# Two transformer and mixer layers on one core: key norms of four head groups in one bank, a third score bank for odd exponential units, score buffers as a ring, and a new order

## The chip, the core and the metric

The kernel runs on one core of a Trainium2 chip. A core has five engines with instruction queues of their own: TensorE (PE; its weight loads are shown as PEld), VectorE (DVE), ScalarE (ACT), GpSimd (POOL) and SyncE (SP), which here issues most of the DMA transfers. Each engine works through its own instructions in the order in which the program has them; between engines there are semaphores. TensorE writes to PSUM, which has eight banks of 128 partitions by 512 float32 numbers. The other memory on the core is SBUF.

The metric is device time in microseconds (us) of one execution, the median of several runs. Before the change it is 1029.02 us over three runs (1027.13 to 1029.56).

## What is computed

Input is one sequence of 2048 tokens with 448 features. A step is an attention block and then a mixer block, each added to its input; two such steps follow each other with the same weights. Called layer 0 and layer 1 below, they are cut here to what matters:

```python
def _A_ref(x, wqkv, wo):                     # 16 heads of 28 columns
    q, k, v = split(x @ wqkv)
    scores = einsum("bhqd,bhkd->bhqk", q, k) * (Dh ** -0.5)
    p = softmax(scores, axis=-1)
    return reshape(einsum("bhqk,bhkd->bhqd", p, v)) @ wo

def _B_ref(x, w1, w2, w3, w4):
    h = gelu(layernorm(x) @ w1)              # 448 columns, in four quarters
    hs = shifted by -1, +1, -2, +2 tokens per quarter @ w2
    x1 = x + hs
    return x1 + gelu(layernorm(x1) @ w3) @ w4   # w3: 448 to 1792

x = x + _A_ref(layernorm(x), wqkv, wo)
x = x + _B_ref(layernorm(x), w1, w2, w3, w4)
x = x + _A_ref(layernorm(x), wqkv, wo)
x = x + _B_ref(layernorm(x), w1, w2, w3, w4)
```

The exponentials of the softmax are 2 layers x 16 heads x 2048 x 2048.

## The kernel before

**Who sets the order.** The kernel isn't written as a list of instructions. Each piece of work is a Python generator (a task) that yields operations, waits for named events, and asks for resources such as a PSUM bank. While the kernel is built, a planner (`Sched`) runs all tasks against planned durations, picks the next operation for each engine, and so fixes each engine's order; `Plan` turns the data dependences into semaphore waits. On the chip the order is fixed, and only the waits decide when an instruction starts. The choices of the planner are steered by tables of constants in the middle of the file: `RANK` (priority of projections, mixer steps and so on), `R_RATE` and `D_RATE` (how many score blocks go to VectorE in which part of the work), `Q_LEAD`, `PE_NORM`, and `XPAR` (thresholds, and by step whether VectorE or GpSimd does it). Where the planner sees TensorE idle, `keep_pe_busy` puts filler matmuls (`filler`, L2165) that compute nothing.

**Tiling.** Tokens are cut into 16 tiles of 128. Four heads form a group, each in 32 of 128 partitions, so there are four head groups. Queries go in chunks of four tiles (512 columns), the last two chunks of each layer in two tiles. `segs` lists the pairs of a query chunk and a head group with a range of key tiles. A segment's scores are cut into blocks of 128 keys by 512 columns (for chunks of two tiles: two key tiles by 256). Over both layers there are 2048 blocks, in the order of the list `stream`.

**The score pipeline.** `t_scores` takes the blocks off the stream in units. An even unit has up to three blocks and the banks 0 to 2, an odd one two blocks and the banks 3 and 4 (`unit_banks`). The scores are row-packed matmuls (L1416). `t_exp` turns a unit into one ScalarE activation (L1654) over all of its banks, into the bf16 buffer `PT` of 15 slots of 512 columns. The planner lets unit u start its scores when the exponential of unit u - 2 has ended. A block's slot is fixed by its unit's number,

```python
home[blk] = ("pt", 5 * ((u // 2) % 3) + 3 * (u % 2) + len(un))
```

so slots are used again after six units, and the exponential of unit u waits until the blocks of unit u - 6 have been used up. Some blocks aren't ScalarE's: in place of an even unit's third block (`ahead_of` with `R_RATE`), or beside a unit in a free bank (`D_RATE`), a later block of the stream is computed by VectorE, as a polynomial with bit operations in five instructions (L1498, two steps at L1525 and L1527, then L1529 and L1532), into `PD` or borrowed space in `vaug`. `t_pv` multiplies the probabilities with the values (L825 is the helper's line for these matmuls), and accumulates in bank 5, which it keeps from start to end. For all other matmuls (projections, mixer, norms; helper line L834) the tasks ask `misc` for one of the banks 6, 7 and 5; bank 5 being held, that leaves 6 and 7. After the last exponential ("tail") all banks are open to them.

**Key norms.** The softmax isn't shifted by the true maximum of a row, but by a bound from the norms of queries and keys. For each layer, each key chunk (`KC`: four chunks in layer 0, five in layer 1) and each head group, `k_proj` projects the keys into a bank, VectorE evacuates them into `kT` (L1182), the squares are formed in `sq` (L1168, on GpSimd or VectorE), one matmul set with `astat` sums them per head in another bank, and VectorE takes the maximum over the tokens (L1195) into `kmaxc`. `t_bias` and `t_bias4` make the biases of the query rows from it (L1325 to L1349). Chunk 0 of layer 0 takes the squares with ScalarE (L1165), for a quick start.

**Other ScalarE work.** The gelus of the mixer: as table gelu in long activations that come after loads of another function table (L2118 for the 1792-wide one, L1916 for the 448-wide one), or, for some chunks, as tanh (L1934), which needs no table load beside exp, with steps on GpSimd and VectorE around it (L1932, L1933, L1935). In the tail the gelus are taken straight from PSUM (L2090, L1898).

**Small steps that are named below.** L2018: GpSimd or VectorE adds the mixer's inner residual. L1763: the attention output is scaled. L1246, L1217, L1438: query rows are evacuated and given their bias. L1262: the values are evacuated into `vaug`. L2149: the output is evacuated into `obf`, two buffers, and stored by a DMA.

Of the kernel before, what the change touches and what calls it, by code (L numbers as in the profile page):

```python
# [184 lines left out]
class Sched:  # L185
# [140 lines left out]
    def keep_pe_busy(self, until):  # L326
# [8 lines left out]
        while True:  # L335
# [21 lines left out]
            if pick is None:  # L357
                if not fits:
                    break
                if self.open5 and all(d.t_end + 0.2 <= t for d in self.P.deps("pe", reads, [key("b5")]).values()):  # L360
                    f_ = self.P.add("pe", lambda e: fn(e, "b5"), reads + [(("xn", 0), "pad")], [key("b5")], t_end=t + dur)
# [190 lines left out]
R_RATE = {(0,): 0, (1,): 0.17, (2,): 0.183, (3,): 0.152, (4,): 0, (5,): 0, (6,): 0.274, (7,): 0.096, (8,): 0.106, (9,): 0.193, (10,): 0.073, (11,): 0.196, (12,): 0.228, (13,): 0, (14,): 0, (15,): 0.457, (16,): 0.306, (17,): 0, (18,): 0, (19,): 0.082, (20,): 0, (21,): 0.089, (22,): 0, (23,): 0.481, (24,): 0, (25,): 0.086, (26,): 0.053, (27,): 0.007, (28,): 0.051, (29,): 0.263, (30,): 0.207, (31,): 0.244, (32,): 0, (33,): 0.012}  # L552
# [3 lines left out]
DWIN = 3.0  # L556
# [5 lines left out]
RANK = {('q', 0, 1): 1, ('q', 0, 2): 1.763, ('q', 0, 3): 1.176, ('q', 1, 0): 1.162, ('q', 1, 1): 1.21, ('q', 1, 2): 1.085, ('q', 1, 3): 1.967, ('b', 0, 0): 3, ('b', 0, 1): 2.77, ('b', 0, 2): 1.853, ('b', 0, 3): 2.798, ('b', 0, 4): 1.211, ('b', 1, 0): 2.781, ('b', 1, 1): 1.849, ('b', 1, 2): 2.32, ('b', 1, 3): 2.579, ('b', 1, 4): 2.042, ('a', 0, 0): 1.98, ('a', 0, 1): 1.742, ('a', 0, 2): 1.882, ('a', 0, 3): 1.528, ('a', 0, 4): 2.263, ('a', 1, 0): 2.618, ('a', 1, 1): 1.108, ('a', 1, 2): 1.44, ('a', 1, 3): 1.223, ('a', 1, 4): 1.214, ('k', 0, 1): 2.594, ('k', 0, 2): 2.273, ('k', 0, 3): 2.136, ('k', 1, 0): 2.166, ('k', 1, 1): 1.68, ('k', 1, 2): 1.231, ('k', 1, 3): 2.338, ('k', 1, 4): 2.507, ('c', 0, 0): 1.464, ('c', 0, 1): 1, ('c', 0, 2): 2.866, ('c', 0, 3): 2.39, ('c', 0, 4): 1.764, ('c', 1, 0): 1.835, ('c', 1, 1): 1.44, ('c', 1, 2): 2.171, ('c', 1, 3): 2.127, ('c', 1, 4): 2.53, ('w', 0, 0): 2.816, ('w', 0, 1): 1.099, ('w', 0, 2): 2.277, ('w', 0, 3): 2.222, ('w', 0, 4): 1.537, ('w', 1, 0): 1.87, ('w', 1, 1): 2.531, ('w', 1, 2): 2.03, ('w', 1, 3): 2.877, ('w', 1, 4): 3, ('o', 0, 0): 2.728, ('o', 0, 1): 1.549, ('o', 0, 2): 1.72, ('o', 0, 3): 1.329, ('o', 0, 4): 2.769, ('o', 1, 0): 2.974, ('o', 1, 1): 3, ('o', 1, 2): 1.615, ('o', 1, 3): 1.476, ('o', 1, 4): 1.611, ('v', 0, 1): 1.389, ('v', 0, 2): 2.811, ('v', 0, 3): 3, ('v', 1, 0): 2.33, ('v', 1, 1): 1.844, ('v', 1, 2): 1, ('v', 1, 3): 1.537, ('v', 1, 4): 2.768, ('l', 1, 0): 1.014, ('l', 1, 1): 1.661, ('l', 1, 2): 2.714, ('l', 1, 3): 2.867, ('l', 1, 4): 1.565}  # L562
Q_LEAD = {(0, 1): 14, (0, 2): 51, (0, 3): 92, (1, 0): 95, (1, 1): 20, (1, 2): 92, (1, 3): 88}
# [36 lines left out]
def build_kernel(nc, A_x, A_wqkv, A_wo, B_x, B_w1, B_w2, B_w3, B_w4, out, n_layers=2):  # L600
# [79 lines left out]
    with st:  # L680
# [489 lines left out]
        def k_proj(L, c, g, xt):  # L1170
# [366 lines left out]
        def t_scores():  # L1537
# [40 lines left out]
            while True:  # L1578
# [32 lines left out]
                if not un:  # L1611
                    break
# [655 lines left out]
```

## Time and profile before

| | |
|---|---|
| median of three runs | 1029.02 us |
| the profiled execution, device time | 1027.56 us |
| its span, from the first to the last instruction | 1025.8 us |
| granted TensorE clock | 1.000 |
| exponentials on ScalarE (L1654) | 356 of 1536 columns, 435 of 1024 |
| first exponential starts, last ends | 16.2 us, 972.7 us |
| filler matmuls (L2165) | 2648 and 644, busy 121.4 and 30.4 us |

Times in the profile are from the span's start. A group's row has line, engine, operation, output and inputs, shape and count, then busy time and the mean of one in ns, then the engine's idle time just ahead of them and what ended it. Busy time counts overlapping instructions once, the mean counts each in full; ScalarE's activations overlap at their ends. A row of the timeline has start, length, group and count, and in brackets the idle time before it and what ended it. A row of the waits has who waited, for whom, the total, the number of times and the longest.

### The profile page before, as it was taken

The numbers are of one execution on the slowest core, as the hardware profiler recorded it, in microseconds if no ns is written. First come the engines' busy times: TensorE is split into PE (matmuls) and PEld (weight loads), VectorE is DVE, ScalarE is ACT, GpSimd is POOL, SyncE is SP. The second block draws the span as 40 slices with busy tenths as digits, with TensorE's granted clock in tenths as the row PEclk, the third lists the DMA queues.
The fourth block names the chain that finished last, engine by engine and source line by source line (L and its number), as shares of the span: only waits on it lengthen the run. The fifth ranks groups of instructions, "written<-read, shape, count | busy, mean of one in ns | idle before, by whom it ended". The sixth has DMA issues, their size and how long they took to land.

```text
span 1025.8 us, 35791 instructions
## 1 busy us (share of the span) xinstructions
PE 973.6 (95%) x16053; PEld 403.7 (39%) x16053; DVE 830.9 (81%) x1616; ACT 982.3 (96%) x903; POOL 255.0 (25%) x370
## 2 busy tenths in 40 slices
PE   8999999999999999999999999999999999899998
PEld 3333344333343334434334333333334333344465
DVE  7977899989869787878788778898999787787652
ACT  7999999999999999999999999999999999999942
POOL 2124132433134204342233111012313020231120
PEclk9999999999999999999999999999999999999999
DMA  4433453311104003231132015334212111121000
GB/s 121 118 90 103 126 166 89 60 33 38 24 26 98 18 14 100 54 54 24 27 91 77 12 62 161 102 73 120 59 29 38 23 47 41 33 64 36 13 21 24
DMA packets 98808, 64.38 MB, mean 63 GB/s; under 512 B 70816, under 2 KB 87536, under 8 KB 98656
## 3 DMA queue, kind: packets, MB, share of 16 engines
q1 hardware_dynamic: 95280, 54.02, 20.4%
q0 software_dynamic: 3376, 8.09, 2.9%
q8 instruction: 125, 2.05, 0.9%
q14 instruction: 27, 0.22, 0.1%
HBM read 28.16 MB, written 16.76 MB: 44 GB/s over the span
## 4 chain that ended last, share of the span: by engine, by line
ACT 73%; PE 23%; DVE 3%; DMA 0%; issue 0%; SPq 0%; DVEq 0%
ACT PT L1654 65%; PE ps L834 13%; PE ps L1416 5%; PE ps L825 4%; ACT h2T L2118 3%; ACT fb L1934 1%; ACT L1654 1%; PE ps L2165 1%; ACT L2118 1%; DMA PT<-in_A_wqkv_dram 0%; ACT sq L1165 0%; ACT vaug L2118 0%; DVE ub L1738 0%; ACT hT L1916 0%; DVE qT L1217 0%
## 5 line engine op out<-in xcount | busy, mean ns | idle before, releaser
L1654 ACT ACTIVATE PT<-ps 128x1024 bf16<-128x1024 f32 (+1 forms) x791 | 887.0, 1316 | 5.4 <-PE ps L1416 4.1
L1416 PE MATMUL ps<-qT,kT 32*128 32x512 bf16 (+1 forms) x2560 | 309.0, 340 | 27.6 <-ACT PT L1654 19.4
L825 PE MATMUL ps<-PT,vaug 128*32 128x512 bf16 (+1 forms) x2428 | 242.4, 341 | 0.1
L1416 PEld LDWEIGHTS ps<-qT,kT 32*128 32x128 bf16 x2560 | 79.3, 91 | 297.3 <-ACT PT L1654 271.1
L834 PE MATMUL ps<-xT,w 128*32 128x512 bf16 (+4 forms) x2592 | 178.6, 343 | 2.8 <-DVE hT L1903 1.5
L2165 PE MATMUL ps<-ident 128*32 128x256 bf16 x2648 | 121.4, 277 | 1.8 <-POOL ident L919 1.5
L825 PEld LDWEIGHTS ps<-PT,vaug 128*32 128x32 bf16 x2428 | 72.0, 95 | 85.8 <-issue 72.6
L834 PEld LDWEIGHTS ps<-xT,w 128*32 128x32 bf16 (+1 forms) x2592 | 69.9, 95 | 53.8 <-issue 24.6
L834 PE MATMUL ps<-w,h2T 128*32 128x448 bf16 x1288 | 86.2, 355 | 4.1 <-ACT h2T L2118 4.0
L2165 PEld LDWEIGHTS ps<-ident 128*32 128x32 bf16 x2648 | 76.3, 97 | 25.7 <-issue 9.9
L1498 DVE TENSOR_SCALAR yd<-ps 128x512 int32<-128x512 f32 x85 | 58.4, 687 | 20.2 <-PE ps L1416 19.1
L2094 DVE CAST h2T<-ps 128x384 bf16<-128x384 f32 (+1 forms) x84 | 51.9, 618 | 24.4 <-PE ps L834 23.7
L1763 POOL TENSOR_TENSOR otn<-ub,fb 128x512 bf16<-128x512 f32 (+1 forms) x24 | 29.4, 1227 | 127.1 <-DMA fb<-rscr 115.1
L1527 DVE SCALAR_TENSOR_TENSOR fb<-fb,yd 128x512 f32<-128x512 f32 x81 | 60.3, 748 | 0.6
L1525 DVE SCALAR_TENSOR_TENSOR fb<-yd 128x512 f32<-128x512 uint16 x81 | 59.6, 741 | 0.5
L1532 DVE SCALAR_TENSOR_TENSOR PD<-yd,PD 128x512 int16<-128x512 int16 x80 | 56.5, 709 | 1.0
L834 PEld LDWEIGHTS ps<-w,h2T 128*32 128x32 bf16 x1288 | 33.7, 96 | 33.2 <-issue 12.4
L1168 POOL TENSOR_TENSOR sq<-qT 128x512 bf16<-128x512 bf16 x20 | 24.4, 1221 | 85.3 <-DVE qT L1217 85.3
L1168 POOL TENSOR_TENSOR sq<-kT 128x512 bf16<-128x512 bf16 (+2 forms) x24 | 22.9, 955 | 90.6 <-DVE kT L1182 62.4
L834 PE MATMUL ps<-xT,wk_pad 128*32 128x512 bf16 (+1 forms) x512 | 42.8, 369 | 0.1
L834 PE MATMUL ps<-wo_pad,otn 128*32 128x448 bf16 x512 | 38.0, 355 | 2.0 <-DVE x_res L1818 1.6
L2007 POOL TENSOR_SCALAR mst<-mv 128x1 f32<-128x1 f32 x32 | 8.5, 268 | 123.7 <-DVE mv L1021 111.4
(210 smaller groups left out, 1319.7 us busy)
## 6 DMA issues: line engine op xcount, KB each, us to landing
uscr<-ub SPq DMA_DIRECT2D x28, 256.0 KB
ub<-uscr SPq DMA_DIRECT2D x28, 256.0 KB, 3.1
fb<-rscr SPq DMA_DIRECT2D x96, 64.0 KB, 2.0
xnd<-xn SPq DMA_DIRECT2D x28, 128.0 KB, 2.0
x_res<-in_A_x_dram POOLq DMA_DIRECT2D x16, 224.0 KB, 4.3
xd<-x_res SPq DMA_DIRECT2D x16, 224.0 KB, 2.2
x_res<-xd SPq DMA_DIRECT2D x16, 224.0 KB, 2.7
out_dram<-obf SPq DMA_DIRECT2D x16, 112.0 KB, 1.7
```

Source lines behind the costliest of these rows:

```text
L825: return lambda e: e.matmul(out=out, lhsT=lhsT, rhs=rhs, start=start, stop=stop, **kw)
L834: r.append(e.matmul(out=out[c:c + w, :], lhsT=lhsT[:, c:c + w], rhs=rhs, start=start, stop=stop, tile_position=(0, c)))
L1168: return both(kp, 0.15 + NW * 0.0018, 0.07 + NW * 0.00052, lambda e: e.tensor_tensor(out=sq[:, si, 0:NW], in0=src, in1=src, op=ALU.mult), ...
L1416: yield op("pe", (0.005 + NW * 0.00042) / nc_, lambda e, i=i, kc=kc, j=j, g=g, a=a, NW=NW, bank=bank: e.matmul(out=ps[:, bank, i * NW:(i + ...
L1498: yield op("dve", c_ps(512), lambda e: e.tensor_scalar(out=y, in0=ps[:, bi(bank), :], scalar1=SCALE * L2E * FS, scalar2=-126.0 * FS, op0=A ...
L1525: yield op(D_[0][0], D_[0][1], lambda e: e.scalar_tensor_tensor(out=q, in0=lo, scalar=E2 / E3 * FS, in1=lo, op0=ALU.add, op1=ALU.mult), re ...
L1527: yield op(D_[1][0], D_[1][1], lambda e: e.scalar_tensor_tensor(out=q, in0=q, scalar=E1 / E3 * FS * FS, in1=lo, op0=ALU.add, op1=ALU.mult) ...
L1532: yield op(D_[3][0], D_[3][1], lambda e: e.scalar_tensor_tensor(out=pdt.bitcast(I16), in0=hi, scalar=128.0, in1=pdt.bitcast(I16), op0=ALU. ...
L1654: yield op("act", 0.0635 + n * w * 0.000833, lambda e, bk=bk, s0=s0, n=n, w=w: e.activation(out=PT[:, s0:s0 + n, 0:w], in_=ps[:, bk[0]:bk[ ...
L2094: ev = op("dve", c_ps(m * NW), lambda e, hr=hr, pv=pv: e.tensor_copy(out=hr, in_=pv), reads=[("ps", bi(b))], writes=hk, touch=[b])
L2118: yield op("act", c_act(len(fr_) * NW), lambda e, v=v: e.activation(out=v, in_=v, func=ACT.Gelu_apprx_tanh), reads=allk, writes=allk, tab= ...
L2165: return [e.matmul(out=ps[32 * c:32 * c + 32, bi(b), 0:256].rearrange("p (a n) -> p a n", n=128), lhsT=xn[:, 0, D:D + 32] if live else ide ...
```

## The change

Key norms: `k_proj` ends with the evacuation, but for chunk 0 of layer 0. A new task `t_knorm` per chunk waits for all four groups, squares each into one of four buffers (two of `sq`, two of `obf`, whose rows grow to 512 columns), sums the four groups with four column-packed matmuls into four quarters of one bank, takes one maximum, spreads it with a small multiplication and a matmul of four columns over the heads, and copies it into `kmaxc`. `t_setup_kn` prepares its constants once. The biases wait for the chunk (`kn`) and no more for the single group.

Scores: the accumulator of `t_pv` moves from bank 5 to bank 7, the free banks are 6 and 5. When fillers made up at least 0.192 of TensorE's last 8 us of the plan, and bank 5 is free, an odd unit takes three blocks and bank 5. Only even units give a third block to VectorE. Slots of `PT` are handed out as a ring of 15, and an exponential waits for the blocks that its slots held last. The block that is given to VectorE is the last free head of a group and no longer the first.

Smaller: `st6` has eight rows used in turn, `vpe` is dropped (its value is written into `rstd`), `dbc`, `db29` and `fct` are smaller, and bank 5 in the list of fillers takes the place of 7. All of the tables that steer the planner have new values.

```diff
+PVBANK = 7
-        MISC = ["b6", "b7", "b5", "b4", "b3", "b2", "b1", "b0"]
+        MISC = ["b6", "b5", "b7", "b4", "b3", "b2", "b1", "b0"]
...
             if not fast:
-                s = yield ("acq", SQ, dk)
-                si = num(s)
-                yield square(("ek", L, c), si, dst, dk, NW)
+                yield ("sig", ("k", L, g, c))
+                return
...
+        def t_knorm(L, c):
...
+            yield ("wait", ("kset",))
+            yield ("acq", ["knorm"])
+            held = []
+            for g in range(4):
+                yield ("wait", ("k", L, g, c))
...
+                s = yield ("acq", ["ob0", "ob1"] + SQ, dk)
...
+                yield both(("ek", L, c), 0.15 + NW * 0.0018, 0.07 + NW * 0.00052, lambda e, buf=buf, src=src: e.tensor_tensor(out=buf, in0=src, in1=src, op=ALU.mult), dk, [key])
+            b = yield misc(*[h[2] for h in held])
+            yield op("pe", max(0.21, c_mm(NW)), lambda e: [e.matmul(out=ps[32 * g:32 * g + 32, bi(b), 0:NW], lhsT=ind8[:, :], rhs=held[g][1], start=True, stop=True, tile_position=(0, 32 * g)) for g in range(4)],
...
+            yield op("dve", c_ps(NW), lambda e: e.reduce_max(out=kmx[:, :], in_=ps[:, bi(b), 0:NW], axis=AX.X), reads=[("ps", bi(b))], writes=[("kmx",)], touch=[b])
+            yield op("dve", 0.13, lambda e: e.tensor_scalar(out=kmd[:, :], in0=indf[:, :], scalar1=kmx[:, 0:1], scalar2=None, op0=ALU.mult), reads=[("kmx",), ("indf",)], writes=[("kmd",)])
+            yield op("pe", 0.12, mm4(ps[:, bi(b), 0:4], astat0[:, :], kmd[:, :], True, True), reads=[("kmd",), ("astat0",)], writes=[("ps", bi(b))], touch=[b], mode="col4", w=0.002)
+            yield op("dve", 0.13, lambda e: e.tensor_copy(out=kmaxc[:, L, :, c], in_=ps[:, bi(b), 0:4]), reads=[("ps", bi(b))], writes=[("kmaxc", L, g, c) for g in range(4)], touch=[b])
...
         def unit_banks(u):
-            return (0, 1, 2)[:len(units[u])] if u % 2 == 0 else (3, 4)[:len(units[u])]
+            return (0, 1, 2)[:len(units[u])] if u % 2 == 0 else (3, 4, 5)[:len(units[u])]
+
+        def place(un, u):
+            n = len(un)
+            if ptr[0] + n > 15:
+                ptr[0] = 0
+            before[u] = sorted(set(x for x in last_user[ptr[0]:ptr[0] + n] if x is not None))
+            for k, blk in enumerate(un):
+                home[blk] = ("pt", ptr[0] + k)
+                last_user[ptr[0] + k] = blk[0:2]
+            ptr[0] += n
...
-                    return (si, kb, js[0])
+                    return (si, kb, js[-1])
...
                 lim = 3 - u % 2
+                if u % 2 == 1 and SC.idle_share(8.0) >= XPAR['wt']:
+                    gw = yield ("try", [["b5"]])
+                    if gw is not None:
+                        widened.add(u)
+                        lim = 3
                 while pos < len(stream) and len(un) < lim:
-                    if len(un) == 2 and rb is None and SC.load("dve", DWIN) < XPAR['dt']:
+                    if len(un) == 2 and u % 2 == 0 and rb is None and SC.load("dve", DWIN) < XPAR['dt']:
...
-                if u >= 6:
-                    for (si, kb, j) in units[u - 6]:
-                        yield ("wait", ("pv", si, kb))
+                for (si, kb) in before[u]:
+                    yield ("wait", ("pv", si, kb))
```

The built program issues, before and after: exponentials of 1536 columns 356 and 362, of 1024 columns 435 and 425; score blocks on VectorE 110 and 112; maxima L1195 36 and 4, the new maximum 0 and 8; tanh steps of 112 x 512 (L1934) 20 and 24; table loads 14 and 14; filler matmuls 3292 and 3304. The first 64 rows of TensorE's list and the first 88 of VectorE's, each a run of equal instructions, are the same in both programs, and so are ScalarE's instructions up to the 18th exponential.

More of the change, by code (lines that the diff above doesn't have):

```diff
@@ L359, in keep_pe_busy @@
                     break
-                if self.open5 and all(d.t_end + 0.2 <= t for d in self.P.deps("pe", reads, [key("b5")]).values()):
-                    f_ = self.P.add("pe", lambda e: fn(e, "b5"), reads + [(("xn", 0), "pad")], [key("b5")], t_end=t + dur)
+                if self.open5 and all(d.t_end + 0.2 <= t for d in self.P.deps("pe", reads, [key("b%d" % PVBANK)]).values()):
+                    f_ = self.P.add("pe", lambda e: fn(e, "b%d" % PVBANK), reads + [(("xn", 0), "pad")], [key("b%d" % PVBANK)], t_end=t + dur)
                     f_.plan = (dur, {"mode": "col4", "w": 0.107})
@@ L1337, in t_bias4 @@
             yield ("wait", ("rtn",))
-            for g in range(4):
-                for c in range(p):
-                    yield ("wait", ("k", L, g, c))
+            for c in range(p):
+                yield ("wait", ("kn", L, c))
             src, sk = kmaxc[:, L, :, 0], [("kmaxc", L, g, 0) for g in range(4)]
```

106 lines of the change are left out of this document (73 added, 33 removed).

## The prediction

> **What bounds the kernel now.** I read the page first: the span, the busy shares, the 40 slices.
>
> ```profile
> span 1025.8 us, 35791 instructions
> PE 973.6 (95%) x16053; PEld 403.7 (39%) x16053; DVE 830.9 (81%) x1616; ACT 982.3 (96%) x903; POOL 255.0 (25%) x370
> PE   8999999999999999999999999999999999899998
> ACT  7999999999999999999999999999999999999942
> L1654 ACT ACTIVATE PT<-ps 128x1024 bf16<-128x1024 f32 (+1 forms) x791 | 887.0, 1316 | 5.4 <-PE ps L1416 4.1
> ```
>
> TensorE and ScalarE both look full, so the shares alone don't decide. The stretches do: columns are length, then busy time of PE, PEld, DVE, ACT and POOL.
>
> ```profile
> 51.30:102.60 51.30, 50.81 (x662) 16.17 (x654) 40.00 (x91) 51.30 (x48) 17.78 (x20) 1.00 0.36 96
> 923.00:974.50 51.50, 49.96 (x890) 23.84 (x890) 37.01 (x77) 51.47 (x52) 7.90 (x16) 1.00 0.10 24
> 1000.00:1025.80 25.80, 22.91 (x507) 13.27 (x496) 5.67 (x9) 7.03 (x15) 2.02 (x2) 1.00 0.07 24
> ```
>
> ScalarE works through whole stretches without a hole; in the last stretch it has 7.03 of 25.80 and TensorE has the work. The waits say which of the two is late in the middle (waiter, releaser, total, times, longest):
>
> ```profile
> ACT PT L1654 <- PE ps L1416: 4.1, 4, 1.8
> ACT qT L1233 <- DVE bc L1332: 0.9, 1, 0.9
> PE ps L1416 <- ACT PT L1654: 19.4, 66, 0.9
> ```
>
> TensorE waits for the exponentials 66 times, they for it four times. TensorE's 95% is partly filler matmuls (L2165), so its slack is larger than the page shows. The kernel is three pieces: a head of 16.2 us until the first exponential, a ScalarE stream until the last one ends at 972.7, and a tail of 53.1 us in which TensorE sets the end. Only what shortens one of the three counts.
>
> The stream's start and its four holes, from ScalarE's timeline (start, length, group, hole before it); its end is the table load at 972.70, quoted with the tail:
>
> ```profile
> 16.20 6.88 ACT L1654 ACTIVATE PT<-ps 128x1536 bf16<-128x1536 f32 x6
> 26.08 2.37 ACT L1654 ACTIVATE PT<-ps 128x1536 bf16<-128x1536 f32 x2 [1.78 <-PE ps L1416]
> 49.07 39.47 ACT L1654 ACTIVATE PT<-ps 128x1536 bf16<-128x1536 f32 x35 [1.07 <-PE ps L1416]
> 105.80 5.97 ACT L1654 ACTIVATE PT<-ps 128x1536 bf16<-128x1536 f32 x5 [0.33 <-PE ps L1416]
> 572.85 2.37 ACT L1654 ACTIVATE PT<-ps 128x1536 bf16<-128x1536 f32 x2 [0.87 <-PE ps L1416]
> ```
>
> **The change part by part: the exponentials.** The listing of both programs' instructions is the count; prices are from the groups kept apart by shape and the chain of waits, where one exponential starts right behind the other:
>
> ```profile
> L1654 ACT ACTIVATE PT<-ps 128x1536 bf16<-128x1536 f32 x356 | 552.5, 1552 | 5.0 <-PE ps L1416 4.1
> L1654 ACT ACTIVATE PT<-ps 128x1024 bf16<-128x1024 f32 x435 | 476.0, 1124 | 0.5
> L1916 ACT ACTIVATE hT<-hT 112x2048 bf16<-112x2048 bf16 x1 | 1.9, 1915 | 0.0
> ```
>
> ```profile
> 414.88 2.25 ACT PT L1654 x2
> 417.66 0.91 ACT PT L1654
> 769.48 1.04 ACT fb L1934 x2
> 955.68 1.34 ACT PT L1654
> ```
>
> The means of 1552 and 1124 ns overlap their neighbours; what one costs the stream is 1.34 and 0.91 us, and a pair 2.25. Before there are 356 wide and 435 narrow ones, after 362 and 425: -10 x 0.91 + 6 x 1.34 = -1.06 us. In blocks of 512 columns that is 1936 instead of 1938; the other 112 of 2048 (before 110) are VectorE's. The third bank for odd units is used by 23 of 393 odd units, while even units give their third block to VectorE 55 times instead of 40. So the wide odd units mostly stand in for narrowed even ones.
>
> The new order also turns one mixer chunk's gelu: the 2048-wide L1916 activation goes (-1.92), four tanh steps of L1934 come (4 x 1.04/2 = +2.08). Table loads stay fourteen. Stream: -1.06 - 1.92 + 2.08 = -0.90 us.
>
> **The key norms.** Rows of the groups, for what goes and what comes:
>
> ```profile
> L1195 DVE TENSOR_REDUCE kmaxc<-ps 128x1 f32<-128x512 f32 (+2 forms) x36 | 22.5, 624 | 5.3 <-PE ps L834 5.2
> L1168 POOL TENSOR_TENSOR sq<-kT 128x512 bf16<-128x512 bf16 (+2 forms) x24 | 22.9, 955 | 90.6 <-DVE kT L1182 62.4 <-PE ps L834 28.2
> L1168 DVE TENSOR_TENSOR sq<-kT 128x512 bf16<-128x512 bf16 (+1 forms) x8 | 3.0, 386 | 0.1
> L1330 DVE TENSOR_SCALAR bcb<-k,sc 128x1 bf16<-128x1 f32 x8 | 1.7, 216 | 0.2
> ```
>
> Thirty-two maxima go and eight come: -24 x 0.624 = -15.0 us of VectorE. Sixteen small steps come, at 0.216 each +3.5. Key squares move: 12 instead of 24 on GpSimd, 20 instead of 8 on VectorE (+12 x 0.386 = +4.6). So VectorE gains 6.9 us, none of it on the chain, for ScalarE waited for a VectorE bias only before the first exponential, and that chunk keeps the old way. What it buys is on the list above: two blocks, 2 x 512 columns of exponential, already counted. The cover is ScalarE's own stream. If a later key chunk's maximum came late (it now needs all four groups and a second matmul), what queues behind it is the bias, then the query rows, then TensorE's scores in their fixed order; nearest price is the hole of 1.07. I take 0, the bound is one such hole per chunk, 8 x 1.07 = 8.6.
>
> **Banks and ring.** An odd unit that takes bank 5 holds it through the exponential ahead and its own, so projections have one free bank instead of two for 2 x 1.34 us. It is taken only where fillers were frequent, so I take 0; if each of the 23 delayed one row of projections by one narrow exponential, 23 x 0.91 = 21 us is the top, and below nothing the gain can't exceed the holes. The ring of 15 buffers puts the wait for old probabilities five to six units back instead of always six, about 5.9 us or more; no wait of ScalarE for L825 stands in the list of before, so 0. The accumulator's move from bank 5 to 7 and the shared or shortened small buffers add no instruction. SyncE issues 440 in both, GpSimd 364 instead of 374.
>
> **Head and tail.** The first 18 exponentials, and TensorE's and VectorE's work behind them, stand in the same order, so the head and the hole of 1.78 stay. Tail rows: ScalarE's steps behind the last exponential, then two TensorE rows of one kind.
>
> ```profile
> 972.70 1.28 ACT L2090 ACT_TABLE_LOAD   x1
> 974.00 1.57 ACT L2090 ACTIVATE kT<-ps 128x512 bf16<-128x512 f32 x3
> 978.53 1.92 ACT L2118 ACTIVATE kT<-kT 128x2048 bf16<-128x2048 bf16 x1
> 984.77 1.92 PE L834 MATMUL ps<-xT,w 128*32 128x256 bf16 x64
> 994.46 4.98 PE L834 MATMUL ps<-xT,w 128*32 128x256 bf16 x176
> ```
>
> After, two instead of three activations of 512 (-0.52) and a joint gelu of 2560 instead of 2048 columns (+1.92/4 = +0.48): nothing. Behind it TensorE has the same groups but 192 instead of 176 of the 256-wide matmuls, at (4.98 - 1.92)/112 = 0.027 us: +0.44. Against that stands 28 fillers put where useful matmuls covered the last normalisation; they run while the gelu is awaited. Tail +0.4, from -1 to +2.
>
> **Sum.** -0.90 + 0.4 = -0.5 on the profiled 1027.56 us, which is 1.46 under the median of 1029.02; on the median's scale 1028.5, if the three movable holes (1.07 + 0.33 + 0.87 = 2.27) are met by others of the same size.
>
> **The rivals.** *Smoother.* A back-to-back stream of before would be 356 x 2.25 + 79 x 0.91 = 872.9 us; the page has 887.0 busy. Part of the 14 is overlap with other activations, part is exponentials that start a little late. Wide odd units give TensorE 1.34 instead of 0.91 us to refill the even banks. With the 2.27 of holes and 2 to 3 of those 14 gone, 1028.5 - 4.5 = 1024. For it: the scores are what the holes wait for. Against: the holes lie where projections crowd TensorE, which is where wide units aren't taken.
>
> *Collisions.* The last hole of before has a story, told in order of time:
>
> ```profile
> 569.36 1.42 POOL L1932 TENSOR_TENSOR fb<-vaug 128x512 f32<-128x512 bf16 x1 [5.28 <-DVE vaug L2087]
> 569.80 1.53 DVE L1935 SCALAR_TENSOR_TENSOR vaug<-fb,vaug 128x512 bf16<-128x512 f32 x1
> 571.92 0.56 PE L834 MATMUL ps<-wv,xT 128*32 128x448 bf16 x8 [0.92 <-DVE vaug L1262]
> ...
> L1935 DVE SCALAR_TENSOR_TENSOR vaug<-fb,vaug x7: 658/681/1529, 549.7 to 610.1; 128x512 bf16<-128x512 f32 x7
> ```
>
> A VectorE step of two buffers runs into a GpSimd one and takes 1.53 instead of 0.68 us; the evacuation behind it is late, TensorE waits 0.92 with the scores queued behind, and ScalarE stands 0.87. The change puts 24 more such two-buffer steps on VectorE (12 key squares, 6 query squares, 6 residual sums) and takes as many from GpSimd, to which eight scalings of L1763 come. In a new order the survivors meet elsewhere. If one in four or five of the 24 meets a GpSimd step ahead of scores, 5 or 6 x 0.87 = +5: 1033.5. It decides from five such meetings on (5 x 0.87 = 4.35, more than the 3.6 that lead from 1028.5 to 1032.1); all 24 would be 1049. Against it: most slow steps of before cost ScalarE nothing, and GpSimd's long steps get fewer.
>
> [...]
>
> *No effect of the parts as such.* The freed VectorE time buys two blocks and the wide units four fewer instructions; with a tail at its upper end the time is 1030.
>
> **How the numbers follow.** A measurement can tell a change of about 0.3%, 3.1 us, from none: 1025.9 to 1032.1. Forecast 1028.5: 0.33. No effect: 0.08. Smoother, 1024: 0.31. Collisions, bank or late key maxima, 1033.5 and up: 0.28. That is faster 0.31, same 0.41, slower 0.28. The likeliest's own range is 1026 to 1031; with one in ten left out on each side, and the gain bounded by 2.27 of holes and part of the 14, I take 1021 to 1037.
>
> **What would show it.** Right: ScalarE's 362 and 425, the last exponential's end near 971.8, a tail near 53.5, and no releaser of more than 2 us in ScalarE's waits besides scores. Smoother: holes under 2.5 in all. Collisions: more holes before L1654, with VectorE steps of 1.5 us ahead of them. Wrong altogether: a first exponential not at 16.2, ScalarE waiting for L825 (the ring) or for a bias, or a tail away from 53 by over 2 us.

## The result, and the profile after

The changed kernel takes 1036.09 us (median of four runs, 1034.64 to 1038.03) against 1028.36 before (1027.13 to 1029.56): a ratio of 1.0076 with a 95% interval of 1.0055 to 1.0098, 7.7 us more. The profiled execution took 1035.85 us. Its page, the span, the busy shares and the row of the exponentials:

```profile
span 1034.1 us, 35682 instructions
PE 974.7 (94%) x15999; PEld 401.2 (39%) x16002; DVE 836.1 (81%) x1646; ACT 982.1 (95%) x901; POOL 245.7 (24%) x360
...
L1722 ACT ACTIVATE PT<-ps 128x1024 bf16<-128x1024 f32 (+1 forms) x787 | 888.2, 1324 | 14.0 <-PE ps L1461 13.4
```

Nothing here looks like 7.7 us of work: ScalarE's busy time is 982.1 (before 982.3), and what stands out is the idle time ahead of the exponentials, 14.0 instead of 5.4. The groups by shape and the list of waits (waiter, releaser, total, times, longest) say the same in two ways:

```profile
L1722 ACT ACTIVATE PT<-ps 128x1536 bf16<-128x1536 f32 x362 | 552.8, 1558 | 11.7 <-PE ps L1461 11.4
L1722 ACT ACTIVATE PT<-ps 128x1024 bf16<-128x1024 f32 x425 | 459.5, 1124 | 2.3 <-PE ps L1461 2.0
```

```profile
ACT PT L1722 <- PE ps L1461: 13.4, 14, 4.3
PE ps L838 <- DMA xT<-xnd: 3.6, 1, 3.6
PE ps L838 <- DVE kmd L1238: 2.9, 2, 2.3
PE ps L829 <- DVE ub L1808: 1.3, 1, 1.3
```

Before, the exponentials waited for scores 4 times, 4.1 us in all. Now it is 14 times and 13.4 us, and TensorE has three waits that the list of before did not show: for a transposing transfer, for the new `kmd` step, and for the evacuation of the accumulator. ScalarE's timeline gives the places (start, length, group and count, the hole before it); the last row is the table load that ends the stream.

```profile
15.63 6.88 ACT L1722 ACTIVATE PT<-ps 128x1536 bf16<-128x1536 f32 x6
...
25.52 2.37 ACT L1722 ACTIVATE PT<-ps 128x1536 bf16<-128x1536 f32 x2 [1.79 <-PE ps L1461]
...
95.33 1.45 ACT L1722 ACTIVATE PT<-ps 128x1536 bf16<-128x1536 f32 x1 [4.28 <-PE ps L1461]
97.09 1.02 ACT L1722 ACTIVATE PT<-ps 128x1024 bf16<-128x1024 f32 x1 [0.30 <-PE ps L1461]
98.60 1.45 ACT L1722 ACTIVATE PT<-ps 128x1536 bf16<-128x1536 f32 x1 [0.49 <-PE ps L1461]
...
390.32 30.46 ACT L1722 ACTIVATE PT<-ps 128x1024 bf16<-128x1024 f32 x28 [1.27 <-PE ps L1461]
...
673.49 67.97 ACT L1722 ACTIVATE PT<-ps 128x1536 bf16<-128x1536 f32 x60 [1.02 <-PE ps L1461]
...
741.96 2.52 ACT L1722 ACTIVATE PT<-ps 128x1536 bf16<-128x1536 f32 x2 [0.50 <-PE ps L1461]
745.55 10.63 ACT L1722 ACTIVATE PT<-ps 128x1536 bf16<-128x1536 f32 x10 [1.07 <-PE ps L1461]
...
980.59 1.28 ACT L2160 ACT_TABLE_LOAD   x1
```

The ledger of the three pieces: head 15.63 (before 16.20), -0.57; stream from 15.63 to 980.59, 964.96 against 956.50, +8.46; tail 1034.1 - 980.59 = 53.5 against 53.1, +0.4; together +8.3, which is the difference of the spans. Of the stream's +8.46 the holes are 13.4 - 4.1 = +9.3, so the work in it became 0.8 us shorter. The added holes lie at four places: A at 95 us (4.28 and followers of 0.30, 0.49 and 0.45, together 5.5), B at 390 (1.27), C at 673 (1.02), D at 742 to 746 (1.57). Beside each of them the granted clock is low. The columns are start and end, length, busy time and count of PE, PEld, DVE, ACT and POOL, then the clock, the mean busy share of the DMA engines, and GB/s:

```profile
84.00:88.00 4.00, 3.76 (x58) 1.24 (x50) 3.71 (x7) 4.00 (x5) 0.00 (x0) 1.00 1.27 178
88.00:92.00 4.00, 1.15 (x17) 0.34 (x17) 2.23 (x5) 3.05 (x3) 0.00 (x0) 1.00 1.19 64
92.00:96.00 4.00, 3.15 (x30) 0.90 (x31) 0.00 (x0) 0.67 (x1) 0.00 (x0) 0.67 0.54 193
384.00:388.00 4.00, 3.50 (x48) 1.34 (x40) 1.62 (x3) 3.97 (x3) 0.00 (x0) 0.64 0.02 4
668.00:672.00 4.00, 2.85 (x31) 1.15 (x32) 4.00 (x9) 4.00 (x4) 0.00 (x0) 0.78 0.33 122
740.00:744.00 4.00, 3.02 (x29) 0.90 (x33) 4.00 (x9) 3.46 (x4) 1.77 (x3) 0.74 0.30 58
```

The kernel before has no stretch of 4 us under 0.97 between 16 us and the tail. Note the rows of 84 to 92 us: the DMA engines are claimed 1.27 and 1.19 times over, and the rate falls from 178 to 64 GB/s. That is place A, and its rows, from the timelines of GpSimd, SyncE and TensorE, are:

```profile
77.41 2.66 POOL L879 DMA_DIRECT2D wo_pad<-in_A_wo_dram  x4 [0.31 <-POOL wo_pad L1029]
...
80.11 0.80 POOL L882 DMA_DIRECT2D w<-in_B_w_dram  x1
80.88 0.60 POOL L883 DMA_DIRECT2D w<-in_B_w_dram  x1
81.46 0.76 POOL L884 DMA_DIRECT2D w<-in_B_w_dram  x1
99.12 1.04 POOL L1231 TENSOR_TENSOR obf<-kT 128x512 bf16<-128x512 bf16 x1 [16.90 <-DVE kT L1200]
...
81.35 3.67 SPq L1171 DMA_TRANSPOSE xT<-xnd  x1
...
92.85 0.40 PE L838 MATMUL ps<-xT,wk_pad 128*32 128x512 bf16 x4 [3.61 <-DMA xT<-xnd]
```

GpSimd issues the weights of the attention output and of the mixer's first half (`wo_pad`, `w1`, `w2`: seven transfers) at 77.41 to 82.2 us. So they now travel beside the transposing transfer that brings the next normalised tokens; it is issued at 81.35, and TensorE, which waits 3.61 us for it with the scores queued behind, starts at 92.85, 11.5 us after the issue. In the kernel before the same loads are issued from 97.86, and the matmul that needs the transfer doesn't wait (GpSimd's and TensorE's timelines):

```profile
97.86 2.66 POOL L875 DMA_DIRECT2D wo_pad<-in_A_wo_dram  x4
...
90.63 0.60 PE L834 MATMUL ps<-xT,wk_pad 128*32 128x512 bf16 x8
```

What moved the loads is an entry of a table. The task that loads the weights waits until the segment numbered `XPAR['l1']` of the score stream starts, and then yields the seven issues; the new tables have 9 there instead of 11:

```diff
-XPAR = {'l0': 6, 'l1': 11, 'l2': 15, ...
+XPAR = {'l0': 10, 'l1': 9, 'l2': 15, ...
```

Built with this one entry back at 11, the changed code puts the seven issues behind the square of 99.12 and leaves every other operation in its place on every engine.

At B and D there is a pair of VectorE and GpSimd, as in the prediction's rival of collisions:

```profile
379.88 1.72 POOL L1833 TENSOR_TENSOR otn<-ub,fb 128x512 bf16<-128x512 f32 x1
380.50 1.64 DVE L1587 SCALAR_TENSOR_TENSOR fb<-fb,yd 128x512 f32<-128x512 f32 x1
382.93 0.19 PE L838 MATMUL ps<-kmd,astat 128*32 128x4 bf16 x4 [2.27 <-DVE kmd L1238]
...
730.87 1.28 POOL L1833 TENSOR_TENSOR otn<-ub,fb 128x512 bf16<-128x512 f32 x1 [10.68 <-PE ps L838]
730.89 1.79 DVE L1585 SCALAR_TENSOR_TENSOR fb<-yd 128x512 f32<-128x512 uint16 x1
740.98 0.60 PE L829 MATMUL ps<-PT,vaug 128*32 128x512 bf16 x5 [1.34 <-DVE ub L1808]
```

### The profile page after: what moved, and what is told of

Its sections match the earlier page's. It is cut to its first block, busy times and chain, and to the rows that moved or that the text cites. A ratio compares the mean times of both kernels' runs of the same rounds, so it can differ in the third digit from the quotient of the medians.

```text
span 1034.1 us, 35682 instructions
## 1 busy us (share of the span) xinstructions
PE 974.7 (94%) x15999; PEld 401.2 (39%) x16002; DVE 836.1 (81%) x1646; ACT 982.1 (95%) x901; POOL 245.7 (24%) x360
## 4 chain that ended last, share of the span: by engine, by line
ACT 63%; PE 28%; DVE 6%; DMA 1%; issue 1%; SPq 0%; POOL 0%; DVEq 0%
ACT PT L1722 57%; PE ps L838 15%; PE ps L1461 7%; PE ps L829 5%; ACT h2T L2188 3%; PE ps L2235 1%; ACT fb L2004 1%; DMA xT<-xnd 1%; DVE fb L1587 1%; ACT L1722 1%; DVE fb L1585 1%; DVE h2T L2164 1%; ACT L2188 0%; DVE PD L1592 0%; DVE x_res L1888 0%
## 5 line engine op out<-in xcount | busy, mean ns | idle before, releaser
L1722 ACT ACTIVATE PT<-ps 128x1024 bf16<-128x1024 f32 (+1 forms) x787 | 888.2, 1324 | 14.0 <-PE ps L1461 13.4
L829 PE MATMUL ps<-PT,vaug 128*32 128x512 bf16 (+1 forms) x2421 | 247.5, 343 | 1.7 <-DVE ub L1808 1.3
L838 PE MATMUL ps<-xT,w 128*32 128x512 bf16 (+4 forms) x2368 | 160.2, 340 | 3.0 <-DVE h2T L2164 1.9
L2235 PE MATMUL ps<-ident 128*32 128x256 bf16 x2472 | 114.1, 280 | 1.5 <-POOL ident L924 1.5
L838 PEld LDWEIGHTS ps<-xT,w 128*32 128x32 bf16 x2368 | 63.1, 95 | 50.9 <-issue 19.8
L2235 PEld LDWEIGHTS ps<-ident 128*32 128x32 bf16 x2472 | 70.9, 98 | 22.9 <-issue 10.4
L1833 POOL TENSOR_TENSOR otn<-ub,fb 128x512 bf16<-128x512 f32 (+1 forms) x32 | 35.6, 1112 | 181.6 <-DMA fb<-rscr 170.7
L1585 DVE SCALAR_TENSOR_TENSOR fb<-yd 128x512 f32<-128x512 uint16 x79 | 54.4, 697 | 0.3
L2235 PE MATMUL ps<-ident,xn 128*32 128x256 bf16 x832 | 42.5, 276 | 0.9 <-DVE ub L1808 0.7
L838 PE MATMUL ps<-xT,wq_pad 128*32 128x512 bf16 x512 | 42.6, 382 | 0.7 <-DVE bc L1378 0.3
L1589 DVE TENSOR_SCALAR PD<-fb 128x512 bf16<-128x512 f32 x86 | 40.1, 471 | 0.9
```

The lines of the kernel that those rows point to most:

```text
L829: return lambda e: e.matmul(out=out, lhsT=lhsT, rhs=rhs, start=start, stop=stop, **kw)
L838: r.append(e.matmul(out=out[c:c + w, :], lhsT=lhsT[:, c:c + w], rhs=rhs, start=start, stop=stop, tile_position=(0, c)))
L1585: yield op(D_[0][0], D_[0][1], lambda e: e.scalar_tensor_tensor(out=q, in0=lo, scalar=E2 / E3 * FS, in1=lo, op0=ALU.add, op1=ALU.mult), re ...
L1589: yield op(D_[2][0], D_[2][1], lambda e: e.tensor_scalar(out=pdt, in0=q, scalar1=E3 / FS ** 3, scalar2=E0, op0=ALU.mult, op1=ALU.add), rea ...
L1722: yield op("act", 0.0635 + n * w * 0.000833, lambda e, bk=bk, s0=s0, n=n, w=w: e.activation(out=PT[:, s0:s0 + n, 0:w], in_=ps[:, bk[0]:bk[ ...
L1833: yield both(("eo", L, ch), 0.2 + NW * 0.0021, 0.07 + NW * 0.00104, lambda e: e.tensor_tensor(out=otn[:, g, 0:NW], in0=u, in1=rb[:, 0:NW], ...
```

## The experiments

All edits but the last two are made behind the planner and ahead of the semaphores, so that every other instruction keeps its place; `place` puts operations of one engine's list ahead of another one, `copies` adds fillers like a given one. The times of the kernel before are those of runs beside it on the same chip; the ratio is estimated from all runs of both kernels, so it isn't simply the quotient of the two medians. Where kernels of different groups are compared, the ratios are the safer guide.

| kernel | median us (range, runs) | before | ratio, 95% interval |
|---|---|---|---|
| e1, weight loads later | 1029.46 (1027.22 to 1030.99, 11) | 1027.71 | 1.0011 (1.0002 to 1.0021) |
| e2, fillers | 1035.04 (1033.33 to 1037.73, 6) | 1027.71 | 1.0072 (1.0058 to 1.0087) |
| e3, GpSimd's products wait | 1032.92 (1030.17 to 1035.71, 6) | 1027.71 | 1.0050 (1.0034 to 1.0067) |
| e4, all three | 1026.11 (1025.88 to 1026.60, 11) | 1027.71 | 0.9981 (0.9972 to 0.9990) |
| f1, before with early loads | 1028.25 (1027.49 to 1030.64, 12) | 1028.04 | 1.0002 (0.9992 to 1.0012) |
| f2, e1 and fillers | 1028.53 (1026.53 to 1030.22, 12) | 1028.04 | 1.0002 (0.9991 to 1.0012) |
| f3, e1 and products wait | 1026.81 (1025.98 to 1028.65, 12) | 1028.04 | 0.9983 (0.9974 to 0.9993) |
| g1, before, w1 and w2 beside the transfer | 1033.20 (1031.65 to 1035.73, 6) | 1027.39 | 1.0058 (1.0045 to 1.0070) |
| g2, loads swapped | 1029.16 (1027.88 to 1030.99, 11) | 1027.39 | 1.0014 (1.0006 to 1.0023) |
| f4, old tables | 1054.37 (1053.92 to 1055.00, 4) | 1028.04 | 1.0251 (1.0233 to 1.0269) |
| f5, no third bank | 1047.52 (1047.30 to 1051.61, 4) | 1027.39 | 1.0202 (1.0185 to 1.0218) |

**e1: the weight loads behind GpSimd's next key square.**

```diff
         est = SC.run()
+        gp = P.ops["pool"]
+        loads = [o for o in gp[26:35] if o.dma]
+        place("pool", loads, gp[36])
```

> The seven weight loads of GpSimd's queue (wo_pad, w1, w2), which the changed kernel issues at 77.41 to 82.2 us, stand behind the key square that ran at 99.12; nothing else moves. Theory: they made the transposing transfer of 81.35 land at 92.85, 11.4 us after its issue where the kernel before took 4.8; with them gone it lands near 86, TensorE's wait of 3.61 us at the wk_pad matmul and the ScalarE hole of 4.28 us at 95.33 go with their followers (0.30, 0.49, 0.45), the clock of 92 to 100 us is back at 1.00, and the kernel takes about 1036.1 - 5.5 = 1030.6 us. Rival (the transfer is late for a reason of its own, its place in SP's queue for one): the wait of about 3.6 us stays, 1036. Rival (the time is given back later, since something behind sets the end): the hole goes, and other holes grow by as much, 1036.

Measured: 1029.46 us, so 6.6 us are gone from 1036.09, a little more than expected. Its operations and their order are those of the changed code with `l1` at 11, so this is also the price of that table entry. The timelines of SyncE and ScalarE in this kernel:

```profile
81.17 1.95 SPq L1171 DMA_TRANSPOSE xT<-xnd  x1
...
733.96 2.48 ACT L1722 ACTIVATE PT<-ps 128x1536 bf16<-128x1536 f32 x2 [0.50 <-PE ps L1461]
737.55 8.37 ACT L1722 ACTIVATE PT<-ps 128x1536 bf16<-128x1536 f32 x8 [1.11 <-PE ps L1461]
```

The transposing transfer is issued at the same time, SyncE is through with it in 1.95 instead of 3.67 us, and no wait for it is left; place A is gone with all its followers. D stands where it was. B and C are not there in this execution, although nothing was done about them: that became the next question.

**e2: fillers where TensorE stood idle.** A filler here is four matmuls that compute nothing.

```diff
+        pe = list(P.ops["pe"])
+        copies(pe[542], 30, pe[545])     # bank 5, ahead of the wk_pad matmul
+        copies(pe[2641], 16, pe[2642])   # bank 5, ahead of kmd
+        copies(pe[5481], 5, pe[4983])    # open bank 7, at 668 us
```

> The changed kernel with more filler matmuls at three places where TensorE stood idle ahead of a low granted clock: 30 (about 3.3 us) into bank 5 ahead of the wk_pad matmul that waits 3.61 us, 16 (1.8 us) into bank 5 ahead of the kmd matmul that waits 2.27 us, 5 into the open bank 7 at 668.4 ahead of scores that wait 0.95 us. The waits stay. Theory (idle TensorE lowers the clock, and the slow matmuls behind it make the later holes): the clock at 92 to 100, 384 to 388 and 668 to 672 us is 0.95 or more; the holes of 0.30, 0.49 and 0.45 behind 95 us, of 1.27 at 390 and of 1.02 at 673 shrink to under a third of that, the hole of 4.28 to about 3.5; sum -3 to -4, about 1032.5 us. Rival (the clock makes nothing late, the waits themselves do): the clock is back and the holes stay, 1036. Rival (the third place's 5 fillers are too few): only the hole at 673 stays, 1033.5.

Measured: 1035.04, 1.0 us less by the medians; by the ratios, 1.0072 against 1.0076, no change that these runs can tell. At A the edit missed its aim. TensorE's timeline of the profiled execution shows why:

```profile
89.11 1.82 PE L2235 MATMUL ps<-ident 128*32 128x256 bf16 x60
94.73 2.17 PE L2235 MATMUL ps<-ident 128*32 128x256 bf16 x60 [3.81 <-issue]
```

In the middle of the fillers, which wait for nothing, TensorE stands for 3.81 us, so that ScalarE's hole there is 8.64 instead of 4.28 us and the clock behind it 0.57. "Issue" is the profile's name for a stop without a wait on record, so here it was not the waits alone that decided when an instruction started. B and C were clean, as they also are in e1, so this kernel by itself doesn't show what the fillers do.

**e3: GpSimd's two products behind the VectorE instruction that they met.**

```diff
+        gp, dv = P.ops["pool"], P.ops["dve"]
+        gp[127].deps["dve"] = dv[658]
+        gp[246].deps["dve"] = dv[1210]
```

> The changed kernel with two products of GpSimd (L1833, at 379.88 and 730.87 us) made to wait for the VectorE instruction that they ran beside (1.64 and 1.79 us, where one alone takes 0.68). Theory (the two slow each other, and VectorE's next ones come late by it): both VectorE instructions take about 0.7 us; the kmd matmul's wait of 2.27 us falls to about 1.3 and the wait for the evacuation at 740.98 (1.34 us) to about 0.3; the holes at 390 (1.27) and 742 to 746 (0.50 and 1.07) shrink by half or more, -1.4 to -2.8, about 1034 us. Rival (VectorE is late by its own load): the holes at 742 to 746 stay, 1035.5 to 1036.

Measured: 1032.92, 3.2 us less than 1036.09 by the medians and 2.7 by the ratios (1.0050 against 1.0076), which is the upper end of what was expected. VectorE's and TensorE's timelines:

```profile
380.97 0.69 DVE L1587 SCALAR_TENSOR_TENSOR fb<-fb,yd 128x512 f32<-128x512 f32 x1
382.17 0.92 DVE L1238 TENSOR_SCALAR kmd<-indf,kmx 128x4 bf16<-128x4 f32 x1
383.14 0.19 PE L838 MATMUL ps<-kmd,astat 128*32 128x4 bf16 x4 [2.01 <-DVE kmd L1238]
...
728.85 0.68 DVE L1585 SCALAR_TENSOR_TENSOR fb<-yd 128x512 f32<-128x512 uint16 x1
737.83 0.60 PE L829 MATMUL ps<-PT,vaug 128*32 128x512 bf16 x5 [0.23 <-DVE ub L1808]
```

At D it went as expected: 1.79 became 0.68, TensorE's wait 1.34 became 0.23, the holes are gone. At B the delayed product now meets the small `kmd` step, which takes 0.92 instead of 0.23, so that TensorE's wait only falls from 2.27 to 2.01. And still there is no hole at B. A wait of over 2 us at that place therefore need not cost ScalarE anything. C isn't there in this execution either, as in e1, without anything being done about it, so part of the gain need not be the edit's.

**e4: the three together** (of the fillers, 8 at B and 5 at C).

> The three edits together: the weight loads behind the square of 99.12, 8 fillers ahead of the kmd matmul and 5 in the open bank at 668.4, and GpSimd's two products behind VectorE. Theory: the four added waits are all of the added time and independent of each other, so the sum of what they cost, 9.4 us of holes, goes but for a small rest: 1036.1 - 8 to 9.4 = 1026.7 to 1028, level with the kernel before or 0.1 to 0.2% below it. Rival (the holes are coupled, what is won at one is lost at the next): 1030 or more.

Measured: 1026.11, 10.0 us under the changed kernel and faster than the kernel before, 0.9981 (0.9972 to 0.9990). Eleven runs lie within 0.7 us, and each shows a clock of 1.000. Stream, from ScalarE's timeline:

```profile
15.76 6.88 ACT L1722 ACTIVATE PT<-ps 128x1536 bf16<-128x1536 f32 x6
970.87 1.28 ACT L2160 ACT_TABLE_LOAD   x1
```

It lasts 955.1 us against 956.5 before, with a tail of 1024.4 - 970.9 = 53.5.

**f2 and f3: the loads later with fillers alone, and with the products' waits alone.** The edits are those of e1, e2 (8 and 5 fillers) and e3.

> The changed kernel with the weight loads behind the square of 99.12 and the fillers (8 ahead of kmd, 5 in the open bank at 668.4), without the waits of GpSimd's products. Beside it the loads alone took 1029.46 us at clocks of 0.995 to 1.000, all three edits 1026.11 at 1.000 in each run. Theory (idle stretches of TensorE lower the clock by chance, each dip 1.3 to 1.6 us; fillers take away the places at 380 and 668, the place at 740 stays): every run at 0.998 or near, none at 0.995, the holes of 0.50 and 1.11 near 735 stay, 1027.5 to 1028.2 us. Rival (only the products' waits matter): 1029.5 as with the loads alone.

> The changed kernel with the weight loads behind the square of 99.12 and GpSimd's two products behind VectorE, without the fillers. Theory: the holes near 735 are gone in each run, the dips of the clock at 380 and 668 come in some runs and not in others: 1026.1 to 1029 with a spread of 2 to 3 us, median 1027 to 1028. Rival (the fillers do nothing): 1026.1 in each run, as with all three edits.

Measured: 1028.53 and 1026.81. With the fillers alone the profiled execution has one low stretch, at D (0.68 and 0.50 from 732 to 740 us, holes of 1.14, 1.14 and 0.39); with the products' waits alone it has one, at C (0.57 from 664 us, a hole of 0.72). So each edit takes away the places that it was meant for and leaves the others. The products' waits are the larger part, 2.65 us on top of e1 by the medians and 2.9 by the ratios; fillers on top of these are worth 0.7 us by the medians and 0.2 by the ratios, which can't be told from nothing. What they do change is the clock: 1.000 in all eleven runs of e4, in five of the twelve of f3. f2 came out 0.3 us above its expectation, and five of its twelve runs have a clock of 0.997, lower than I had expected for one place.

The runs' own clocks order the times. For e1: 1027.22 us at 1.000, 1027.84 and 1028.15 at 0.998, 1029.28 to 1029.67 at 0.997, 1030.06 to 1030.99 at 0.995. It is one program in one order, and its clock is lower in one execution than in the next.

**f1, g1, g2: is it the weights beside the transfer?** f1 moves the loads in the kernel before, `w1` and `w2` ahead of a square at 78.19, `wo_pad` into GpSimd's free stretch from 83.6.

```diff
+        gp = list(P.ops["pool"])
+        loads = [o for o in gp[33:40] if o.dma]
+        place("pool", loads[4:7], gp[27])
+        place("pool", loads[0:4], gp[30])
```

> The kernel before, with its old key norms; only the seven weight loads of GpSimd's queue are issued earlier: w1 and w2 ahead of the key square of 78.19 us, wo_pad in the queue's free stretch from 83.6 (they stood at 97.86 to 102.6). Theory (these transfers hold up the transposing one): it is issued at about 82 as before and lands near 90 to 93 instead of 87; TensorE, which first uses it at 90.63, waits up to 3 us, a hole of the same size stands in ScalarE's stream near 92, and the time is 1029 to 1033. Rival (in the changed kernel the transfer was late by something else of the new order): it lands by 88, no wait at 90.63, and the time stays at 1027.7; the two squares that start 1.2 to 1.5 us later cost at most that.

Measured: 1028.25, no change; the theory as I had put it missed. The 392 KB of `w2`, the last of the three issues, landed in 4.4 us, from an issue at 78.58, that is, by 83, while the transposing transfer was only issued at 82.27. Early loads as such cost nothing. What f1 lacked was the overlap of `w1` and `w2` with the transfer. g1 makes it, in the kernel before, and g2 takes most of it away in the changed one (`w2`, issued at 78.84, lands there 4.7 us later), by nothing more than swapping `wo_pad` with `w1` and `w2`:

```diff
+        place("pool", gp[37:40], gp[29])     # g1, in the kernel before
```
```diff
+        place("pool", gp[32:35], gp[27])     # g2, in the changed kernel
```

> The kernel before, with w1 and w2 (three issues, 784 KB) ahead of the key square of 82.58 us, so that they are issued at about 80.6 to 82.7, beside the transposing transfer of 82.0 as in the changed kernel; wo_pad stays at 97.86. With w1 and w2 at 77.0 to 79.3 and wo_pad at 84.0 nothing was late: they had mostly landed before the transposing began. Theory (w1 and w2 in flight together with the transposing transfer hold each other up, as in the changed kernel, where the engines were 1.1 to 1.4 busy at 50 to 140 GB/s from 86 to 92 us): the first w takes 8 us or more to land instead of 4.4, the rate from 84 to 90 us falls under 150 GB/s, TensorE waits 1 to 6 us at 90.6, and the time is 1030 to 1033 us. Rival (it takes something of the changed kernel's own, such as its slab load right behind the transposing issue): landing in 5 us, no wait, 1028.

> The changed kernel with the same seven loads in the same stretch of GpSimd's queue, but w1 and w2 (784 KB) first, at 77.4 to 79.6 us, and wo_pad behind them, at 79.6 to 82.2. Theory (it is w1 and w2 in flight beside the transposing transfer of 81.35): they land by about 83, the transfer is late by 2 us at most, TensorE's wait of 3.61 us falls under 1, and the time comes near that of the loads moved away, 1029.5 to 1031 us. Rival (any of the seven, or all bytes together): the wait stays at 2.5 us or more, 1034 to 1036.

Measured: g1 1033.20, g2 1029.16. The landing of `w2` from the lists of DMA issues (count, size, median us to landing), for the changed kernel, f1 and g1 in this order:

```profile
w<-in_B_w_dram POOLq DMA_DIRECT2D x1, 392.0 KB, 10.8
```
```profile
w<-in_B_w_dram POOLq DMA_DIRECT2D x1, 392.0 KB, 4.4
```
```profile
w<-in_B_w_dram POOLq DMA_DIRECT2D x1, 392.0 KB, 9.4
```

TensorE's timelines of g1 and of g2, and, from the table of stretches, g1's DMA:

```profile
93.14 0.61 PE L834 MATMUL ps<-xT,wk_pad 128*32 128x512 bf16 x8 [2.89 <-DMA xT<-xnd]
...
89.40 0.40 PE L838 MATMUL ps<-xT,wk_pad 128*32 128x512 bf16 x4
...
88.00:92.00 4.00, 2.25 (x35) 0.54 (x25) 1.82 (x3) 3.31 (x4) 0.00 (x0) 1.00 1.18 193
```

The kernel before, which has none of the change, shows the wait at the same matmul and loses 5.8 us; the changed kernel, with the same seven loads in the same 5 us of GpSimd's queue, is rid of place A. It isn't any load beside the transfer, then: in g2 `wo_pad` (392 KB in four issues) goes out from 79.59 to 81.94, with the transfer at 81.58, and in f1 from 84.04, 1.8 us behind it, and TensorE doesn't wait. One detail of g1's expectation failed: the rate stayed near 200 GB/s, at a busy share of 1.18, so the collapse to 64 GB/s in the changed kernel isn't needed for the transfer to be late.

**f4 and f5: parts of the change in an order found anew.** f4 is the changed code with the tables of the kernel before, f5 the changed kernel with the threshold of the third bank out of reach.

```diff
-XPAR = {'l0': 10, 'l1': 9, ... 'wt': 0.192}
+XPAR = {'l0': 10, 'l1': 9, ... 'wt': 9.0}
```

> The changed kernel's code (joint key norms, ring, lending of the third bank) with the tables of the kernel before (rates, ranks, leads, norm shares, and the starts and places in XPAR), so that the order is found with the old settings; nine key squares of the first layer stand ahead of the weight loads on GpSimd again. Theory (the added time hangs on where the order put the loads and not on the joint norm as such): no late transposing transfer, no hole of more than 2 us near 95; the sum is 1026 to 1031 by what other holes an order with untuned settings leaves. Rival (the joint norm itself is late and costs, one longer chain for each of ten chunks): 1033 or more, with holes behind kmd matmuls.

> The changed kernel without the lending of the third bank: the odd exponential units stay 1024 wide, and the order is found again with the tables otherwise as they are. What is known of it: ScalarE then has as many 1536 and 1024 units as before (about +1.1 us), and the weight loads still go out early. Theory (the late transfer is independent of the lending): a hole of 3 to 6 us near 95 stays, 1034 to 1040 us by what else the new order brings. Rival (the lending takes the fillers' bank and so costs the 7 us): 1030 or less.

Measured: 1054.37 and 1047.52; neither expectation held. In f4, with `l1` at 11 again, the loads stand behind the key squares in GpSimd's order, and as expected no wait of TensorE for a transposing transfer is on the list; but ScalarE's timeline has large holes at the seams of chunks and layers; the largest is

```profile
760.59 21.48 ACT L1722 ACTIVATE PT<-ps 128x1024 bf16<-128x1024 f32 x19 [7.49 <-PE ps L829]
```

while TensorE waits for `kmd` only twice, 1.1 us in all, so the rival of late key norms is not borne out either. In f5, with `l1` at 9, the loads go out at 77 to 82 us, 3.3 us and more ahead of the transposing transfer at 85.36; no wait for it appears and the hole near 95 is missing. That agrees with g1 and g2, but isn't what I had expected of this kernel. The lesson of the pair is a limit. A code whose tables were not fitted to it loses 20 to 26 us, several times the price of any part, so parts can't be priced by planning anew.

## Why the prediction failed, by its steps

*Counts and prices of the exponentials, and the tail: right.* 362 and 425 exponentials; the work in the stream shrank by 0.8 us where -0.90 was forecast; the tail is 53.5, as forecast.

*The head: 15.63 instead of 16.20.* ScalarE waited 0.66 us for the first weights' load instead of 1.24, and that is not the change: in g1, which has the old code there, the first hole's row starts at 25.53 too (before 26.08). As a sign of being wrong altogether it was a bad choice.

*The step that failed: the sum has no term for where the new tables put the DMA issues.* The prediction compared them by number ("SyncE issues 440 in both, GpSimd 364 instead of 374") and priced key squares as engine time, but nowhere asked when the loads go out. Through `l1` seven of them moved up by 20.4 us (97.86 to 77.41) into the flight of a transfer for which TensorE waits with scores behind it. This is 6.6 of the 10.0 us that the edits win back (by ratios to the kernel before, 1.0076 becomes 1.0011), shown by undoing it (e1), by swapping the order of the same loads (g2) and by making it in the kernel before (g1). That GpSimd has fewer key squares isn't the reason: with `l1` at 11 the changed code has as few of them, and its loads go out late again, as in e1. The condition that the sum was given, that the movable holes "are met by others of the same size", was where it entered: the holes are 13.4 us and not 4.1. That 1036.09 still lies within 1021 to 1037 is luck: the upper end came from the rivals' terms, and place A is in none of them.

*Key norms, priced at 0 with 8.6 as the bound.* The chain that I named did become late once, 2.27 us at B. It cost 1.27 in the changed kernel's profile, where the clock fell to 0.64 behind it, and nothing in e1, with the same wait of 2.26 us. So 0 to 1.3 us in all, by the execution.

*Banks and ring.* No wait of ScalarE for the old probabilities appears, as forecast for the ring. At C both free banks are taken (bank 5 by a wide unit, bank 6 by a block for VectorE) and the accumulator is being evacuated, so no filler had a place; TensorE is busy 2.85 of 4 us there, at a clock of 0.78, and in e1 2.66 of 4 us at 1.00. That the lending is the reason was read from the order and not tried by itself.

*Collisions, the rival.* Its mechanism is there, at two meetings, where five were asked for. Beside GpSimd's product a VectorE step takes 1.64 us at B and 1.79 at D, against 0.69 and 0.68 once they are kept apart; the product itself takes 1.72 and 1.28 against 1.26 and 1.27, so at D VectorE's step alone is longer. Keeping them apart is worth 2.65 us (f3 against e1), 2.9 by the ratios. e3 adds that at B the delay only moved on to the next VectorE step that the product met, `kmd`, 0.92 instead of 0.23. The rival's 1033.5 came closer to the measured time than the forecast, but mostly for a reason that it didn't contain.

*Smoother, the rival.* With the four places mended, the stream is 1.4 us shorter than before, 0.9 of it forecast work. What is left for smoother scores is about half a microsecond, not 4.5.

So with its four places mended the change is worth 1.6 us by the medians, 2.0 by the ratio (e4; 0.5 was forecast), and the order found for it gave back 10. Part of the 1.6 is the steady clock: eight of the 23 runs of the kernel before beside it have a clock under 1.000, none of e4's.

## What to carry to other kernels

When an order is found anew, compare not only how many instructions each queue has but where its DMA issues stand: here a load that went out earlier, beside a transfer on the critical path, cost 6.6 us (e1). A load that nobody needs yet can be made to wait behind an instruction that already marks the right time, or simply be issued in another order. Where TensorE stands idle for a microsecond or two, as here for 0.95 to 2.27 us, read the granted clock of that stretch and of several runs before a late wait is blamed.

## What the runs showed of the hardware

The transposing transfer and the loads of `w1` and `w2` were late beside each other. In the kernel before such a transfer lands 4.8 us after its issue (median of 13). With `w1` and `w2` (784 KB) issued within 1.5 us of it, TensorE had it 11.5 us after the issue in the changed kernel and 11.7 in g1, and `w2` itself took 9.3 (e3) to 14.3 us (e2) instead of 4.4 (f1). With the same loads issued 2.7 to 5.3 us ahead of it (g2, f1) TensorE didn't wait, nor did it with `wo_pad` close to it (79.59 to 81.94 us in g2, the transfer at 81.58). Why `w1` and `w2` hold it up and `wo_pad` doesn't, and what they share with it, is not shown.

The stop of 3.81 us amid e2's fillers falls into this stretch. Among the DMA queues the page lists two for instructions; from 88 to 96 us one of them (q8) had a single packet, which took 1.8% of 16 engines' 8 us, 2.3 us, against 0.8 to 1.0% in the kernel before, e1 and g1, which also have one packet there. Whether TensorE's stop comes from that was not tried.

TensorE's clock fell after idle stretches as short as 0.95 us (C, where TensorE was busy 2.85 of 4 us) and 1.34 us (D), and it fell in some executions only: at B the same wait went with a clock of 0.64 in the changed kernel (2.27 us) and 1.00 in e1 (2.26), and C, with TensorE busy 2.85 and 2.66 of 4 us, with 0.78 and 1.00. What decides it is not shown; the eleven runs of e1, one program, spread over 3.8 us at clocks from 0.995 to 1.000. The holes beside a dip at B, C or D came to 0.7 us (f3, at C) to 2.7 (f2, at D).
